# A fused linear-attention and two-layer MoE kernel: routing by groups of six chunks, rows written chunk by chunk from ScalarE's queue, row tiles in the ring of PSUM banks, two conversions on ScalarE

## The chip, the cores and the metric

The kernel runs on one core of one Trainium2 chip. The metric is the device time of one execution in microseconds (us). Before the change the median of three runs is 537.44 us (537.41 to 537.68).

## What is computed

The reference, cut to what matters (4 sequences, 8 heads, 768 steps, head size 48; 3072 tokens of width 384, 8 experts of width 1024):

```python
for t in range(S):                                   # linear attention
    state = alpha[:, :, t, :, None] * state + einsum('bhd,bhe->bhde', k[:, :, t], v[:, :, t])
    y[:, :, t] = einsum('bhd,bhde->bhe', q[:, :, t], state)
x = y.transpose(0, 2, 1, 3).reshape(B * S, H * D)    # 3072 x 384

# MoE 1, only where x @ w_skip > 0; other tokens keep x
e = argmax(x @ w_gate); gate = softmax(x @ w_gate)[e]
x = x + gate * (relu(x @ w1[e]) @ w2[e])

# MoE 2, all tokens, no residual
e = argmax(x @ w_gate2); gate = softmax(x @ w_gate2)[e]
out = gate * (relu(x @ w1b[e]) @ w2b[e])
```

## The kernel before

The work has three stages: the scan with the routing (up to about 160 us), the experts of the first MoE, the experts of the second. The change lies in the first.

The scan handles 24 chunks (NB) of 128 tokens, six for each sequence. The loop at L744 is software-pipelined: iteration g holds pieces of several chunks, and each engine takes its instructions in the order in which they are written. In iteration g stand, one behind the other:

- emit_a(g+1): the products of keys and queries, ap0 and ap1 on PE (L566), each into a bank of PSUM; the causal mask of the first on VectorE (DVE, L574), that of the second on ScalarE (a copy, ACT L571) and GpSimd (POOL L572). Then the keys are transposed on PE (kp, L581) and copied out by ScalarE (ks, L583), except for a sequence's last chunk.
- prep(g+3): the decays. Two scans on DVE (pp L546, qka L550), a reciprocal between them (L548), and two multiplications on POOL (L554, L555).
- emit_y(g): PE adds up the new state (sp, L599, L610, L611) and the chunk's result (yp, L605, L606, L614, L615). ScalarE copies y out (L618), DVE writes the carried state s (L621), which PE reads in the next iteration.
- emit_r(g-1): PE turns y into the tokens' rows of 384 columns and 17 logits (rp, L642). ScalarE copies the rows (xr, L643), DVE adds up the logits (lg, L644).
- the loads of later chunks, v (g+3) and qka (g+5), on SP's queue, which also loads the experts' weights.

PSUM: ap, sp and yp are taken from a ring of four banks ("B"), by the pool as they come free. kp and rp share one further bank ("K", a single buffer), so that kp of an iteration waits until the readers of rp ahead of it have ended: xr on ScalarE, and lg on DVE. Two readers of one bank are also kept apart from each other: lg follows xr. Small routing values lie in one more bank ("own", by spot()).

Routing: the tokens of a group of chunks (GROUPS, eight groups of three) are routed together, by the generator route(i) at L648: cm (L655, L656), a softmax over 8 experts for both layers (L264 to L278; the exponential is ACT's L269), the one-hot choice ohm (L660), the counts and gates (L328 to L289), rank (PE matmuls rk, L312 to L315), positions (L342 to L360), the tables mv (L365) and hot (L372), and the index matmul idx_ps (PE, L377). A group's columns of rows, gate, token number and second logits stand in one tile xr, and SP writes it to the table xrows in DRAM, 394 floats a token (L679). The generators are stepped an instruction at a time by rt() calls between the base instructions of DVE, and how many steps an iteration gets stands in the table RT (L51). Each step is one or a few DVE instructions. Half-weight conversions of the experts (L207, on DVE or POOL) are put in between by release() and background().

After chunk 17 (SPLIT = 6 groups of three) the first index is read and the first expert's rows are gathered by POOL (L441), while the last six chunks go on; after the last chunk the others follow. A gather reads whole rows of xrows, so the writes must have landed.

The constants of the routing are converted in iteration 0, at L757 to L769, on DVE: upper and ones to 16 bit, and small tables copied to PSUM.

Of the kernel before, what the change touches and what calls it, by code (L numbers as in the profile page):

```python
# [8 lines left out]
F32 = mybir.dt.float32  # L9
# [3 lines left out]
AF = mybir.ActivationFunctionType  # L13
ALU = mybir.AluOpType
# [32 lines left out]
GROUPS = [3] * 8  # L47
SPLIT = 6
# [60 lines left out]
def body(tc, qka, vN, rw, wg2, wg17, w1a, w2a, w1b, w2b, cst, zr, out):  # L109
# [3 lines left out]
    with ctx:  # L113
# [21 lines left out]
        with ExitStack() as fctx, tc.manual_schedule():  # L135
# [125 lines left out]
            def softmax_pick(l, n, w, res, scale=1.0):  # L261

                mx = spot("mx", 6, n, w)
                V.tensor_reduce(mx, l, axis=AX.X, op=ALU.max)  # L264
                yield 0
                sh = sm.tile([128, n, w, 8], F32, tag=f"sh{w}", name="sh")
                V.tensor_tensor(sh, l, mx.rearrange("p a (b o) -> p a b o", o=1).to_broadcast([128, n, w, 8]), op=ALU.subtract)
                ex = sm.tile([128, n, w, 8], F32, tag=f"ex{w}", name="ex")
                A.activation(out=ex, in_=sh, func=AF.Exp, scale=scale)  # L269
                yield 0  # L270
                eq = sm.tile([128, n, w, 8], F32, tag=f"eq{w}", name="eq")
                de = kept["desc"].rearrange("p (a e) -> p a e", a=1).to_broadcast([128, n * w, 8])
                V.scalar_tensor_tensor(out=eq.rearrange("p a b e -> p (a b) e"), in0=sh.rearrange("p a b e -> p (a b) e"),
                                       scalar=0.0, in1=de, op0=ALU.is_ge, op1=ALU.mult)
                yield 0
                V.tensor_reduce(mx, eq, axis=AX.X, op=ALU.max)
                yield 0
                V.tensor_tensor(eq, eq, mx.rearrange("p a (b o) -> p a b o", o=1).to_broadcast([128, n, w, 8]), op=ALU.is_equal)  # L278
                res += [eq, ex]
                yield 0  # L280

            def gates(ex, n, w, res):
                den = spot("den", 6, n, w)
# [55 lines left out]
            def index(i, n, nl, ohm, on, rk, cols, region, first, last):  # L339
# [12 lines left out]
                tl = spot("tl", 3, n, 1)  # L352
                V.tensor_reduce(tl[:, :, 0], ge, axis=AX.X, op=ALU.add)
                yield 0
                ti = spot("ti", 24, n, 2, 4)
# [3 lines left out]
                pm = sm.tile([128, n, 1], F32, tag=f"pm{nl}", name="pm")  # L359
# [12 lines left out]
                V.tensor_tensor(hot, kept["iota"].rearrange("p (o c) -> p o c", o=1).to_broadcast([128, n, 128]), pm.to_broadcast([128, n, 128]), op=ALU.is_equal)  # L372
# [261 lines left out]
            def emit_r(g):  # L634

                i, k, n, _ = gof[g]
                if k == 0:
                    xr[i] = em.tile([128, n, ROW], F32, tag="xr", name="xr", bufs=3)
                y = st.pop(("ys", g))
                rp = bank("B" if g == NB - 1 else "K", "rp", NP, 113)  # L640
                for p in range(NP):
                    T.matmul(rp[:, p, :], lhsT=y[:, p, :], rhs=rws[:, p, :], start=True, stop=True)  # L642
                A.activation(out=xr[i][:, k, 0:DM].rearrange("p (a b) -> p a b", a=NP), in_=rp[:, :, 0:96], func=AF.Copy)  # L643
# [4 lines left out]
            def route(i):  # L648
# [5 lines left out]
                cm = spot("cm", 6, n, 2, 1)  # L654
# [9 lines left out]
                def row_ends():  # L664
# [10 lines left out]
                    V.tensor_reduce(x[:, :, GATE], den, axis=AX.X, op=ALU.add)  # L675
                    V.tensor_copy(x[:, :, TOK], kept["tok"][:, g0:g0 + n])
                    V.tensor_tensor(x[:, :, LOG:], l[:, :, 9:17], kept["one"].rearrange("p (a o) -> p a o", o=1).to_broadcast([128, n, 8]), op=ALU.mult)
                    yield 0
                    SY.dma_start(xrows[1 + g0 * 128:1 + (g0 + n) * 128, :].rearrange("(k p) d -> p k d", p=128), x)  # L679
# [64 lines left out]
            for g in range(NB):  # L744
# [11 lines left out]
                if g == 0:  # L756
                    V.tensor_copy(upper, cc("upper"))  # L757
                    V.tensor_copy(ones, cc("ones"))
                    for name, w in (("desc", 8), ("tok", NB), ("iota", 128), ("seq", 8)):
                        kept[name] = spot(name, w, w, bufs=1)  # L760
                        V.tensor_copy(kept[name], cc(name))
# [464 lines left out]
```

## Time and profile before

| | |
|---|---|
| median of three runs | 537.44 us |
| the profiled execution's own time | 539.43 us |
| its span, first to last instruction | 537.70 us |
| PE busy | 496.3 us (92%), 4704 matmuls |
| PE weight loads busy | 381.6 us (71%) |
| DVE busy | 371.5 us (69%), 1031 instructions |
| ScalarE busy | 256.4 us (48%), 466 |
| POOL busy | 262.3 us (49%), 226 |
| granted TensorE clock, mean | 0.981 |

The shares are means over three stages with different limits, so the stage of the scan is read by itself. The page slices the span in 40 (13.4 us each): DVE is at nine tenths or above from the third slice to the tenth, PE at eight tenths or above. From the thirteenth on, DVE falls to three to six tenths and PE stays at nine, which is the stage of the experts. Busy times of PE end where the profile's model puts a matmul's end.

### The profile page before, as it was taken

Reading aid. Unit: us, or ns where it says so; the run is one execution under the profiler, and the core shown is the slowest. Engines: PE = TensorE matmul, PEld = TensorE weight load, DVE = VectorE, ACT = ScalarE, POOL = GpSimd, SP = SyncE. Lnnn points to the kernel's source line nnn. Section 1 sums busy time; section 2 is a strip of 40 time slices with the busy share of each in tenths; the row PEclk is TensorE's granted clock in tenths of the full one; section 3 lists DMA queues with packets and bytes.
Section 4 is the critical chain, followed back from the end, with each engine's and each line's share of the span. In section 5 each row is a group of like instructions: output and inputs, shape, how many; then the busy total and the mean of one; then the engine's idle time right before and its main releaser. Section 6 shows DMA issues by size and latency. Waiting matters only on the chain.

```text
span 537.7 us, 12030 instructions
## 1 busy us (share of the span) xinstructions
PE 496.3 (92%) x4704; PEld 381.6 (71%) x4704; DVE 371.5 (69%) x1031; ACT 256.4 (48%) x466; POOL 262.3 (49%) x226
## 2 busy tenths in 40 slices
PE   5889898998988999999879989999999999999993
PEld 3678787877877899989879757465555566666662
DVE  7978999999876868888768846863636364646320
ACT  1324343444433566566556415653546364646420
POOL 2366958668625666876947341416215150402121
PEclk9989999999999999999989999999999999999997
DMA  8756877425246667676874158473444535360010
GB/s 304 258 190 209 314 250 264 159 114 208 82 173 209 198 249 229 218 260 199 301 245 145 41 196 275 149 244 123 165 147 140 176 118 208 103 223 28 16 39 26
DMA packets 41460, 96.74 MB, mean 180 GB/s; under 512 B 3641, under 2 KB 28471, under 8 KB 41398
## 3 DMA queue, kind: packets, MB, share of 16 engines
q1 hardware_dynamic: 36662, 82.40, 45.0%
q0 software_dynamic: 4736, 13.51, 7.3%
q8 instruction: 39, 0.64, 0.5%
q14 instruction: 23, 0.19, 0.1%
HBM read 83.41 MB, written 12.99 MB: 179 GB/s over the span
## 4 chain that ended last, share of the span: by engine, by line
PE 56%; DVE 28%; DMA 5%; issue 5%; POOL 2%; ACT 2%; POOLq 0%; DVEq 0%; ACTq 0%
PE hp L464 8%; PE hp L463 8%; PE hp L465 8%; DVE pp L546 6%; DVE qka L550 5%; PE ypc L487 4%; PE ypc L488 4%; PE ypc L489 4%; DMA raw<-in_w1a 3%; PE yp L489 3%; PE yp L488 3%; PE yp L487 3%; PE tp L450 3%; POOL w0l L207 2%; DVE at L574 1%
## 5 line engine op out<-in xcount | busy, mean ns | idle before, releaser
L978 POOL DMA_INDIRECT out<-o,ixo x31 | 31.3, 1009 | 142.2 <-ACT o L1051 125.2
L469 DVE SCALAR_TENSOR_TENSOR h2l<-hp,h2h 128x352 f16<-128x352 f32 (+8 forms) x66 | 38.6, 585 | 64.0 <-ACT h2h L468 63.2
L465 PE MATMUL hp<-x2h,w0l 128*128 128x352 f16 (+8 forms) x216 | 68.7, 323 | 0.0
L463 PE MATMUL hp<-x2h,w0h 128*128 128x352 f16 (+8 forms) x216 | 68.7, 323 | 0.0
L464 PE MATMUL hp<-x2l,w0h 128*128 128x352 f16 (+8 forms) x216 | 68.7, 323 | 0.0
L207 POOL TENSOR_TENSOR w1l<-raw,w1h 128x768 bf16<-128x768 f32 (+1 forms) x26 | 43.0, 1681 | 28.2 <-ACT w1h L202 13.7
L463 PE MATMUL hp<-xh,w0h 128*128 128x200 f16 (+7 forms) x216 | 54.0, 257 | 2.5 <-DVE hl L469 1.4
L468 ACT ACTIVATE h2h<-hp 128x352 f16<-128x352 f32 (+8 forms) x66 | 33.8, 513 | 46.9 <-PE hp L465 45.2
L202 ACT ACTIVATE w0h<-raw 128x768 f16<-128x768 f32 x64 | 53.4, 836 | 4.6 <-DMA raw<-in_w1a 2.7
L441 POOL DMA_INDIRECT xg<-xrows,ix x41 | 49.1, 1197 | 11.6 <-issue 9.8
L464 PEld LDWEIGHTS <-w0h 128*128 128x128 f16 x432 | 43.0, 100 | 16.3 <-issue 3.0
L464 PE MATMUL hp<-xl,w0h 128*128 128x200 f16 (+7 forms) x216 | 53.9, 257 | 0.5 <-DVE xl L452 0.3
L465 PEld LDWEIGHTS <-w0l 128*128 128x128 bf16 x432 | 43.0, 100 | 15.6 <-issue 0.7
L465 PE MATMUL hp<-xh,w0l 128*128 128x200 f16 (+7 forms) x216 | 53.9, 257 | 0.0
L488 PE MATMUL yp<-hl,w1h 128*128 128x200 f16 (+7 forms) x216 | 53.4, 255 | 0.5 <-DVE hl L469 0.5
L487 PE MATMUL yp<-hh,w1h 128*128 128x200 f16 (+7 forms) x216 | 53.5, 255 | 0.0
L202 ACT ACTIVATE w1h<-raw 128x768 f16<-128x768 f32 x64 | 51.5, 836 | 4.1 <-DMA raw<-in_w2a 3.8
L489 PE MATMUL yp<-hh,w1l 128*128 128x200 f16 (+7 forms) x216 | 53.4, 255 | 0.0
L463 PEld LDWEIGHTS <-w0h 128*128 128x128 f16 x432 | 43.0, 100 | 13.6 <-issue 0.5
L554 POOL TENSOR_TENSOR qka<-qka 128x512 f32<-128x512 f32 (+1 forms) x24 | 27.5, 1147 | 47.1 <-DVE qka L550 35.7
L207 DVE TENSOR_TENSOR w0l<-raw,w0h 128x768 bf16<-128x768 f32 x38 | 39.7, 1044 | 14.4 <-ACT w0h L202 12.2
L207 POOL TENSOR_TENSOR w0l<-raw,w0h 128x768 bf16<-128x768 f32 (+1 forms) x26 | 43.2, 1685 | 5.0 <-ACT w0h L202 3.8
(183 smaller groups left out, 1346.2 us busy)
## 6 DMA issues: line engine op xcount, KB each, us to landing
qka<-in_qka SPq DMA_DIRECT2D x21, 772.0 KB, 6.0
raw<-in_w1a SPq DMA_DIRECT2D x8, 1536.0 KB, 6.6
raw<-in_w2a SPq DMA_DIRECT2D x8, 1536.0 KB, 9.4
raw<-in_w1b SPq DMA_DIRECT2D x8, 1536.0 KB, 7.9
raw<-in_w2b SPq DMA_DIRECT2D x8, 1536.0 KB, 7.0
xrows<-xr SPq DMA_DIRECT2D x8, 591.0 KB, 3.7
v<-in_vN SPq DMA_DIRECT2D x24, 192.0 KB, 5.1
xrows<-x SPq DMA_DIRECT2D x9, 197.0 KB, 4.1
```

Source lines behind the costliest of these rows:

```text
L202: A.activation(out=hi[:, sl], in_=r[:, sl], func=AF.Copy)
L207: eng.tensor_tensor(lo[:, sl], r[:, sl], hi[:, sl], op=ALU.subtract)
L441: P.indirect_dma_start(out=dst, out_offset=None, in_=xrows[0:rows], in_offset=bass.IndirectOffsetOnAxis(ap=ix, axis=0), bounds_check=rows ...
L463: T.matmul(hp[:, i], lhsT=wh[:, k, f], rhs=xh[:, k, 0:n], start=(k == 0), stop=False)
L464: T.matmul(hp[:, i], lhsT=wh[:, k, f], rhs=xl[:, k, 0:n], start=False, stop=False)
L465: T.matmul(hp[:, i], lhsT=wl[:, k, f], rhs=xh[:, k, 0:n], start=False, stop=(k == 2))
L468: A.activation(out=hh[:, f0:f0 + nf, 0:n], in_=hp, func=AF.Relu)
L469: V.scalar_tensor_tensor(out=hl[:, f0:f0 + nf, 0:n], in0=hp, scalar=0.0, in1=hh[:, f0:f0 + nf, 0:n], op0=ALU.max, op1=ALU.subtract)
L487: T.matmul(yp, lhsT=wh[:, f, ds], rhs=hs[0][:, f, c0:c1], start=(f == 0), stop=False)
L488: T.matmul(yp, lhsT=wh[:, f, ds], rhs=hs[1][:, f, c0:c1], start=False, stop=False)
L489: T.matmul(yp, lhsT=wl[:, f, ds], rhs=hs[0][:, f, c0:c1], start=False, stop=(f == 7))
L546: V.tensor_tensor_scan(pf, a, bz, initial=0.0, op0=ALU.mult, op1=ALU.add)
```

## The change

Four edits, all in the scan stage.

1. GROUPS is [6, 6, 6, 3, 3] and SPLIT is 3, so that the first 18 chunks are three groups and not six. The spots for routing values in PSUM are twice as large. pm moves from SBUF to PSUM, and iota is no longer copied to PSUM: hot compares the constant in SBUF with pm.
2. rp is taken from the ring of four banks, and kp has the bank K alone.
3. ScalarE copies a chunk's 384 columns to a tile xy of its own (four buffers) and starts the DMA that writes them to xrows. The group's tile xr holds the last ten columns alone, 40 bytes a token, which SP writes.
4. The conversions of upper and ones stand on ScalarE.

```diff
-GROUPS = [3] * 8
-SPLIT = 6
+GROUPS = [6, 6, 6, 3, 3]
+SPLIT = 3
...
-                mx = spot("mx", 6, n, w)
+                mx = spot("mx", 12, n, w)
...
-                pm = sm.tile([128, n, 1], F32, tag=f"pm{nl}", name="pm")
+                pm = spot("pm", 6, n, 1)
...
-                V.tensor_tensor(hot, kept["iota"].rearrange("p (o c) -> p o c", o=1).to_broadcast([128, n, 128]), pm.to_broadcast([128, n, 128]), op=ALU.is_equal)
+                V.tensor_tensor(hot, cc("iota").rearrange("p (o c) -> p o c", o=1).to_broadcast([128, n, 128]), pm.to_broadcast([128, n, 128]), op=ALU.is_equal)
...
                 if k == 0:
-                    xr[i] = em.tile([128, n, ROW], F32, tag="xr", name="xr", bufs=3)
+                    xr[i] = em.tile([128, n, ROW - DM], F32, tag="xr", name="xr", bufs=3)
                 y = st.pop(("ys", g))
-                rp = bank("B" if g == NB - 1 else "K", "rp", NP, 113)
+                xy = em.tile([128, DM], F32, tag="xy", name="xy", bufs=4)
+                rp = bank("B", "rp", NP, 113)
                 for p in range(NP):
                     T.matmul(rp[:, p, :], lhsT=y[:, p, :], rhs=rws[:, p, :], start=True, stop=True)
-                A.activation(out=xr[i][:, k, 0:DM].rearrange("p (a b) -> p a b", a=NP), in_=rp[:, :, 0:96], func=AF.Copy)
+                A.activation(out=xy.rearrange("p (a b) -> p a b", a=NP), in_=rp[:, :, 0:96], func=AF.Copy)
+                A.dma_start(xrows[1 + g * 128:1 + (g + 1) * 128, 0:DM], xy)
...
-                    V.tensor_reduce(x[:, :, GATE], den, axis=AX.X, op=ALU.add)
-                    V.tensor_copy(x[:, :, TOK], kept["tok"][:, g0:g0 + n])
+                    V.tensor_reduce(x[:, :, GATE - DM], den, axis=AX.X, op=ALU.add)
+                    V.tensor_copy(x[:, :, TOK - DM], kept["tok"][:, g0:g0 + n])
...
-                    SY.dma_start(xrows[1 + g0 * 128:1 + (g0 + n) * 128, :].rearrange("(k p) d -> p k d", p=128), x)
+                    SY.dma_start(xrows[1 + g0 * 128:1 + (g0 + n) * 128, DM:].rearrange("(k p) d -> p k d", p=128), x)
...
-                    V.tensor_copy(upper, cc("upper"))
-                    V.tensor_copy(ones, cc("ones"))
-                    for name, w in (("desc", 8), ("tok", NB), ("iota", 128), ("seq", 8)):
+                    A.activation(out=upper, in_=cc("upper"), func=AF.Copy)
+                    A.activation(out=ones, in_=cc("ones"), func=AF.Copy)
+                    for name, w in (("desc", 8), ("tok", NB), ("seq", 8)):
```

Lines behind L642 shift by one or two: lg is L646 after the change, xy L644, its DMA L645.

How the instructions stand, at three places. First DVE at the end of iteration 0; the names are those of tiles, out <- in. Before:

```order
L621 TENSOR_TENSOR s<-sp,pp 128x192
L757 CAST upper<-cs 128x128
L758 CAST ones<-cs 128x128
L761 COPY own<-cs 128x8
L761 COPY own<-cs 128x24
L761 COPY own<-cs 128x128
```

The same engine and place after the change:

```order
L621 TENSOR_TENSOR s<-sp,pp 128x192
L763 COPY own<-cs 128x8
L763 COPY own<-cs 128x24
L763 COPY own<-cs 128x8
L766 COPY own<-cs 128x4
```

Two conversions and the copy of iota have left the row. They stand now on ScalarE, ahead of iteration 1's mask copy, where also the first xy and its DMA are seen, at the end of iteration 1:

```order
L618 ACTIVATE y<-yp 112x512
L759 ACTIVATE upper<-cs 128x128
L760 ACTIVATE ones<-cs 128x128
L571 ACTIVATE at<-ap_271 128x512
L583 ACTIVATE ks<-kp 128x512
L618 ACTIVATE y<-yp 112x512
L644 ACTIVATE xy<-rp 128x384
L645 DMA xrows<-xy 128x384
```

The DMA stands behind the copy it waits for, and ahead of the next iteration's mask copy and ks.

Second, DVE where a group's table hot is done and the next chunks follow. Before, at the end of the routing of chunks 3 to 5, in iteration 8:

```order
L372 TENSOR_TENSOR hot<-own,pm 128x384
L207 TENSOR_TENSOR w0l_727<-raw_0_490,w0h_726 128x768
L574 TENSOR_TENSOR at<-ap_916,cs 128x512
L546 SCALAR_TENSOR_TENSOR pp<-qka,bz 128x520
L548 RECIPROCAL bz_113<-pp 128x4
L550 SCALAR_TENSOR_TENSOR qka<-qka,bz_113 128x520
L621 TENSOR_TENSOR s<-sp,pp 128x192
L644 TENSOR_REDUCE lg<-rp 128x17
L655 TENSOR_SCALAR own<-lg 128x3
L656 TENSOR_SCALAR own<-lg 128x3
L264 TENSOR_REDUCE own<-lg 128x6
L574 TENSOR_TENSOR at<-ap_992,cs 128x512
```

After, at the end of the routing of chunks 0 to 5, also in iteration 8:

```order
L372 TENSOR_TENSOR hot<-cs,own 128x768
L207 TENSOR_TENSOR w0l_688<-raw_0_492,w0h_687 128x768
L574 TENSOR_TENSOR at<-ap_883,cs 128x512
L546 SCALAR_TENSOR_TENSOR pp<-qka,bz 128x520
L548 RECIPROCAL bz_113<-pp 128x4
L550 SCALAR_TENSOR_TENSOR qka<-qka,bz_113 128x520
L621 TENSOR_TENSOR s<-sp,pp 128x192
L646 TENSOR_REDUCE lg<-rp 128x17
L574 TENSOR_TENSOR at<-ap_961,cs 128x512
L546 SCALAR_TENSOR_TENSOR pp<-qka,bz 128x520
```

Before, the next group begins with the next chunk. After, routing stands in iterations 6 (three instructions), 7 (eleven) and 8 (thirteen), then in none up to the end of iteration 12, where the next group begins; that one stands in 13 to 15, and the third in 19 and 20. From chunk 20 on, the order is that of before except for widths. Weight splits (L207) stand at the ends of iterations 8, 12, 16 and 20.

Third, PE around chunk 10, with what each instruction waits for (Activation is ScalarE, Pool GpSimd, DMAHW a DMA queue). Before:

```order
L642 MATMUL rp<-rws,y 128x113 [waits Activation_49]
L642 MATMUL rp<-rws,y 128x113 x3
L566 MATMUL ap_916<-qka 128x128 [waits DMAHW6_49,Pool_49]
L566 MATMUL ap_917<-qka 128x128 [waits DVE_49]
L566 MATMUL ap_916<-qka 128x128
L566 MATMUL ap_917<-qka 128x128
L566 MATMUL ap_916<-qka 128x128
L566 MATMUL ap_917<-qka 128x128
L566 MATMUL ap_916<-qka 128x128
L566 MATMUL ap_917<-qka 128x128
L581 MATMUL kp<-cs,qka 128x128 [waits DVE_49]
L581 MATMUL kp<-cs,qka 128x128 x3
```

After:

```order
L643 MATMUL rp<-rws,y 128x113 [waits Activation_49]
L643 MATMUL rp<-rws,y 128x113 x3
L566 MATMUL ap_883<-qka 128x128 [waits DMAHW1_49,DVE_49,Pool_49]
L566 MATMUL ap_884<-qka 128x128 [waits DVE_49]
L566 MATMUL ap_883<-qka 128x128
L566 MATMUL ap_884<-qka 128x128
L566 MATMUL ap_883<-qka 128x128
L566 MATMUL ap_884<-qka 128x128
L566 MATMUL ap_883<-qka 128x128
L566 MATMUL ap_884<-qka 128x128
L581 MATMUL kp<-cs,qka 128x128 [waits Activation_49]
L581 MATMUL kp<-cs,qka 128x128 x3
```

kp waited for DVE in every iteration; after the change it waits for ScalarE (ks of the chunk before) or for nothing. In about 12 of the last 20 iterations one or both of the ap tiles wait for DVE, which has to read the bank's last tile first.

## Rows read from the trace of the kernel before

**Rows 1.** Windows by stage: bounds, length, busy PE, PEld, DVE, ACT, POOL (instructions); clock, DMA share, GB/s.

```profile
34.00:54.40 20.40, 20.18 (x283) 17.36 (x280) 16.41 (x48) 9.26 (x18) 12.48 (x15) 1.00 0.71 246
54.40:124.10 69.70, 64.03 (x887) 54.99 (x886) 67.91 (x182) 30.66 (x57) 50.52 (x40) 1.00 0.63 222
124.10:153.20 29.10, 27.27 (x377) 23.50 (x376) 24.12 (x82) 12.92 (x26) 18.41 (x16) 1.00 0.36 128
```

**Rows 2.** All of L581 (kp): what PE idled for, us and times.

```profile
  DVE lg L644: 16.8, 21
```

**Rows 3.** Timeline of DVE, iterations 0 and 1: start us, duration us, engine, line, operation, tiles.

```profile
21.44 1.18 DVE L757 CAST upper<-cs 128x128 f16<-128x128 f32 x1
22.54 1.22 DVE L758 CAST ones<-cs 128x128 f16<-128x128 f32 x1
...
25.31 0.69 DVE L574 TENSOR_TENSOR at<-ap,cs 128x512 f32<-128x512 f32 x1
...
28.80 0.22 DVE L644 TENSOR_REDUCE lg<-rp 128x17 f32<-128x68 f32 x1
```

**Rows 4.** Timeline of PE, same stretch; in brackets the idle time before and its releaser.

```profile
29.07 1.04 PE L581 MATMUL kp<-cs,qka 128*128 128x128 f32 x4 [1.87 <-DVE lg L644]
```

**Rows 5.** Groups of PE instructions, 54.4 to 124.1: count, busy us, mean ns, idle before.

```profile
L377 PE MATMUL idx_ps<-mv,hot 128*128 128x96 f16 x15 | 1.5, 209 | 0.2
...
L315 PE MATMUL rk<-cum,ones 128*128 128x48 f16 x4 | 0.7, 183 | 0.0
```

**Rows 6.** Groups of DVE instructions by form, 20 to 160 us, columns as before.

```profile
L546 DVE TENSOR_TENSOR_SCAN pp<-qka,bz 128x520 f32<-128x520 f32 x20 | 31.3, 1565 | 0.0
L550 DVE TENSOR_TENSOR_SCAN qka<-qka,bz 128x520 f32<-128x520 f32 x21 | 29.0, 1379 | 0.6
L574 DVE TENSOR_TENSOR at<-ap,cs 128x512 f32<-128x512 f32 x20 | 13.6, 681 | 0.4 <-PE ap L566 0.3
L621 DVE TENSOR_TENSOR s<-sp,pp 128x192 f32<-128x192 f32 x20 | 6.8, 338 | 0.2
L644 DVE TENSOR_REDUCE lg<-rp 128x17 f32<-128x68 f32 x24 | 5.3, 220 | 6.7 <-ACT xr L643 6.7
...
L548 DVE RECIPROCAL bz<-pp 128x4 f32<-128x4 f32 x20 | 3.5, 176 | 0.3
...
L365 DVE TENSOR_TENSOR mv<-on,own 128x192 f16<-128x192 f16 x7 | 2.4, 346 | 0.0
...
L365 DVE TENSOR_TENSOR mv<-on,own 128x96 f16<-128x96 f16 x7 | 1.7, 242 | 0.0
```

**Rows 7.** Timeline of DVE in a later iteration, around chunk 15.

```profile
105.59 2.65 DVE L546 TENSOR_TENSOR_SCAN pp<-qka,bz 128x520 f32<-128x520 f32 x1
...
109.68 0.33 DVE L621 TENSOR_TENSOR s<-sp,pp 128x192 f32<-128x192 f32 x1
```

**Rows 8.** All of L679 (SP writes xr): ns min/median/max, first and last start; landing.

```profile
L679 SPq EVENT_SEMAPHORE x8: 4868/9852/13631, 40.2 to 155.5; - x8
L679 SPq DMA_DIRECT2D xrows<-xr x8: 383/394/399, 48.8 to 160.4; - x8
...
DMA to landing us min/median/max: 3.4/3.7/5.4
```

**Rows 9.** Timeline of all engines, 33.5 to 41 us: ScalarE and DVE in one iteration.

```profile
35.27 0.49 ACT L643 ACTIVATE xr<-rp 128x384 f32<-128x384 f32 x1 [0.41 <-PE rp L642]
35.79 0.23 DVE L644 TENSOR_REDUCE lg<-rp 128x17 f32<-128x68 f32 x1 [2.23 <-ACT xr L643]
...
36.45 0.60 ACT L571 ACTIVATE at<-ap 128x512 f32<-128x512 f32 x1 [0.70 <-PE ap L566]
```

**Rows 10.** Timeline of POOL at the end of the stage: the gather behind the last write.

```profile
166.13 1.02 POOL L441 DMA_INDIRECT xg<-xrows,ixb  x1 [8.80 <-DVE own L700]
```

**Rows 11.** Timeline of PE in the iteration of rows 7.

```profile
108.52 1.16 PE L566 MATMUL ap<-qka 64*128 64x128 f32 x16
```

More of the change, by code (lines that the diff above doesn't have):

```diff
@@ L282, in gates @@
             def gates(ex, n, w, res):
-                den = spot("den", 6, n, w)
+                den = spot("den", 12, n, w)
                 V.tensor_reduce(den, ex, axis=AX.X, op=ALU.add)
@@ L350, in index @@
                 yield 0
-                tl = spot("tl", 3, n, 1)
+                tl = spot("tl", 6, n, 1)
                 V.tensor_reduce(tl[:, :, 0], ge, axis=AX.X, op=ALU.add)
                 yield 0
-                ti = spot("ti", 24, n, 2, 4)
+                ti = spot("ti", 48, n, 2, 4)
                 V.tensor_tensor(ti, cc("seq")[:, 0:4].rearrange("p (a o e) -> p a o e", a=1, o=1).to_broadcast([128, n, 2, 4]),
@@ L653, in route @@
                 res = []
-                cm = spot("cm", 6, n, 2, 1)
+                cm = spot("cm", 12, n, 2, 1)
                 V.tensor_scalar(cm[:, :, 0, :], l[:, :, 0:1], 0.0, None, op0=ALU.is_gt)
@@ L674, in row_ends @@
                     yield 0
-                    V.tensor_reduce(x[:, :, GATE], den, axis=AX.X, op=ALU.add)
-                    V.tensor_copy(x[:, :, TOK], kept["tok"][:, g0:g0 + n])
-                    V.tensor_tensor(x[:, :, LOG:], l[:, :, 9:17], kept["one"].rearrange("p (a o) -> p a o", o=1).to_broadcast([128, n, 8]), op=ALU.mult)
+                    V.tensor_reduce(x[:, :, GATE - DM], den, axis=AX.X, op=ALU.add)
+                    V.tensor_copy(x[:, :, TOK - DM], kept["tok"][:, g0:g0 + n])
+                    V.tensor_tensor(x[:, :, LOG - DM:], l[:, :, 9:17], kept["one"].rearrange("p (a o) -> p a o", o=1).to_broadcast([128, n, 8]), op=ALU.mult)
                     yield 0
-                    SY.dma_start(xrows[1 + g0 * 128:1 + (g0 + n) * 128, :].rearrange("(k p) d -> p k d", p=128), x)
+                    SY.dma_start(xrows[1 + g0 * 128:1 + (g0 + n) * 128, DM:].rearrange("(k p) d -> p k d", p=128), x)
                 side = [start(row_ends())]
```

## The prediction

> **What bounds the kernel now.** I read the windows by stage first, then the order of the instructions, then the timelines of single iterations. The change lies in the first 160 us, where the scan loop runs with its routing, so only those stages count.
>
> The windows begin where a chunk's rp begins. From 34.0 to 54.4 us, four iterations, PE is busy 20.18 of 20.40 us and DVE 16.41: PE sets the pace, at 20.2 / 4 = 5.05 us an iteration [rows 1]. From 54.4 to 124.1, twelve iterations and four routing groups, DVE is busy 67.91 of 69.70 and PE 64.03: DVE sets the pace and PE has 5.7 us of waiting, nearly all of it in front of the kp transposes, which wait for DVE's logit reduction lg (16.8 us in 21 waits over the whole loop) [rows 1, 2]. From 124.1 to 153.2 both have holes, PE 1.8 us and DVE 5.0 [rows 1]. Behind 153.2 stand the expert networks, which the change leaves as they are.
>
> So a gain must be a DVE instruction less where DVE is full, or a PE wait less where PE is not. An iteration is a loop in lockstep: PE's ap feeds DVE's mask, and the carried state s, at the end of DVE's share, feeds the next matmuls. Neither engine can run a whole iteration ahead of the other.
>
> **Part 1: the constants converted on ScalarE (start).** In iteration 0 DVE converts upper and ones, 1.18 and 1.22 us, and copies the constants behind them; its next mask starts at 25.31 [rows 3]. A little later PE stands 1.87 us in front of kp, until lg is done at 28.80 + 0.22 us [rows 3, 4]. After the change the DVE row runs from s straight to the small copies, shorter by 2.4 us and by the iota copy. ScalarE takes the two conversions while it waits for PE. kp waits for lg no more, as rp leaves its bank, so PE can gain the 1.87 us of that wait and not much more. Value −1.9; bounds 0 (something else of DVE's is late there) and −2.7 (all that DVE is spared).
>
> **Part 2: fewer groups of routing.** *Iterations 3 to 6 (34.0 to 54.4 us).* PE-bound, and the first group's rank and index matmuls are gone from them: idx is 1.5 us for 15, so 0.3 for a group, and one kind of rank matmul 0.7 us for four, 0.18 each, of which a group has four [rows 5]: about 1.0 together, partly under neighbours. Value −0.4, bounds 0 and −1.0.
>
> *Iterations 7 to 18 (54.4 to 124.1).* A chunk's share of DVE: scans 1.565 and 1.379, mask 0.681, state 0.338, lg 0.220, reciprocal 0.176 us, together 4.36 [rows 6]. Instructions overlap: 21.44 + 1.18 is 22.62, and the next starts at 22.54 [rows 3]; six times 0.08 off leaves 3.9 a chunk, 46.8 for twelve. Of the 67.9 busy us [rows 1] 21.1 remain: three weight splits that the order puts there, taken at a scan's 1.3 each, and four groups, 4.3 us a group. A group of six costs more per instruction: mv takes 242 ns for 96 columns and 346 for 192 [rows 6], 1.08 ns a column; hot grows by 384 columns, mv by 96 and 192, on by 96, the dozen softmax and rank tensors by 48 or less, some 1,340 columns or 1.45 us. So a group of six costs 5.75 where two of three cost 8.6: DVE is spared 2.85 us per six chunks, 5.7 in all.
>
> What reaches the end is less, since the order makes the load uneven. Routing is stepped out at the old rate, so a group of six is through after about three iterations, and the other three have base work alone. With the in-place base at 4.0 (the scans stretched a little) the routing iterations of the first six take 3 × 4.0 + 5.75 + a split of 1.3 = 19.05, DVE-bound; the other three fall to PE's 5.05 each, 15.15. Together 34.2. The second six has its three routing iterations at 19.5 and comes to 34.65. Sum 68.85 for 69.70: value −0.9. Bounds −5.7, if the slack evens out across iterations, and +3, if scans stretch as the one of 2.65 us did [rows 7].
>
> *From iteration 19.* The group of chunks 12 to 17 is now six wide: +1.45 us of DVE where three wide stood. DVE is busy 24.12 of 29.10 there [rows 1], so part is hidden: +0.9, bounds 0 and +1.45. The last two groups of three are as before.
>
> **Part 3: rows and logits in the ring of banks.** The wait of kp for lg, 16.8 us in 21 [rows 2], goes. It is not a saving of 16.8: where DVE is full, PE waits for DVE a few matmuls later instead. Its share at the start is in part 1; elsewhere 0, bounds inside those of part 2. The price is that five tiles an iteration share four banks where four did. By the order ap then waits for a DVE reader in some 12 of the last 20 iterations. That is the slower rival below; 0 here.
>
> **Part 4: rows written from ScalarE's queue.** 24 more DMA issues on ScalarE; one on SP's queue takes 383 to 399 ns [rows 8]. Behind each stand the next at (the second half's mask copy) and ks. ScalarE is busy 30.66 of 69.70 us [rows 1], and after xr it idles 0.70 us for ap before at [rows 9], longer than an issue. Value 0; the bound, all of them on the path, is 24 × 0.4 = +9.6, taken far off since the row shows the cover. If the ring makes ap late, the cover grows.
>
> The group's remaining write is now 40 bytes a token, 768 pieces for six chunks. On SP's queue the write waits 4.9 to 13.6 us for the routing, with loads behind it [rows 8]; there are five such waits now for eight, and the row of loads runs ahead by two chunks or more: 0. The old write landed after 3.4 to 5.4 us, the last issued at 160.4 [rows 8]; the gather that needs it is issued at 166.13 [rows 10]. Even 5.4 gives 165.8: 0; bound +1.7, for a landing of twice the median (160.4 + 7.4 − 166.1). The Trainium skill, DMA: Bandwidth & Descriptors, § Specifications, puts the size for full rate at 512 bytes and over, with a read-modify-write below; by it the landing would lie nearer that bound, and the sum would be up to 1.7 more. No row here shows writes as small as these.
>
> hot now reads iota from SBUF and pm from PSUM, still one operand in PSUM as the mask has, whose 681 ns for 512 [rows 6] is the usual rate: 0.
>
> **Sum.** −1.9 − 0.4 − 0.9 + 0.9 = −2.3. The profiled execution took 539.43 us, 2.0 above the median; −2.3 gives 537.1 against it and **535.1** against the median of 537.44.
>
> **Rivals.**
>
> *PE has more room than its busy time says.* Then all 5.7 us of DVE's saving counts in place of 0.9: 535.1 − 4.8 = 530.3. For it: PE's weight loads are busy 54.99 of 69.70 only [rows 1], and PE's 5.7 us of waiting are just as many. Against it: at 34.0 to 54.4 us iterations take 5.05 us with PE never waiting and DVE waiting 2.23 in one place [rows 1, 9]. The Trainium skill, Perfetto Trace Analysis, § Identifying the Most-Contended Engine, calls matmul busy time a poor measure and weight-load busy share a better one; by it PE is at 79% and this rival holds. The trace speaks against it with the 5.05 us. Chance 0.17.
>
> *The ring of banks, slower.* A loop closes through the banks: ap waits until s, the last of DVE's chunk, has read its bank; then ap, mask, scan, scan, s. In one iteration before, ap starts at 108.52 and s ends at 109.68 + 0.33, 1.5 us later [rows 7, 11]: ap could run ahead of s, and with the ring it can't. That exposes ap's time, which one piece of a timeline has at 1.16 us [rows 11], in iterations bound by DVE. Six of the twelve have routing, and with 12 in 20 that is 3.6 waits, 3.6 × 1.16 = +4.2: 539.3. It decides from the point where such a loop passes PE's 5.05: 1.16 + 0.6 + scan + 0.1 + 1.3 + 0.3, so from a first scan of 1.6 us, about the mean of today's [rows 6]. Against it: s has moved earlier in the iterations without routing, and banks are taken as they come free, so that not every loop closes. Chance 0.18.
>
> *The unevenness eats it.* Iterations with routing lose what the others win, and at the start another wait takes half of the 1.9: −0.9 + 0 + 0.9, so 537.4, no change. For it: PE-bound iterations were already within 1 us of DVE's. Chance 0.22.
>
> **How the numbers follow.** Forecast 0.43, around 533 to 537. A measurement here tells about 0.2% from no change, 1.1 us. Faster: 0.37 of the forecast's, all 0.17 of the first rival's and 0.03 of the third's, 0.57. Slower: 0.16 of the ring's, 0.01 of the third's. Same: the rest, 0.26. The range goes from the first rival's 530.3 to 540.0, past the ring's 539.3; half of either rival and the forecast's tail lie outside, under 0.2.
>
> **What would show it.** Part 1: no PE wait in front of kp near 29 us, and the fifth rp at 52 instead of 54.4. Part 2: rp to rp near 6.3 us in routing iterations and 5.05 in the others, about 68.9 for the twelve. Part 3: waits of PE ap for DVE s; if they add up to several us, the ring rival holds. Part 4: the ScalarE queue shows no wait between its DMA and at, and the small write lands before the last gather. I am wrong if iterations without routing also take 5.5 us or more, or if they fall well below 5.

## The result and the profile after

Measured together on one chip, eight runs each, the kernel before takes 538.64 us (median, 537.41 to 540.39) and the changed one 533.74 (532.96 to 535.38). The ratio is 0.9912, 95% interval 0.9897 to 0.9927: 4.7 us faster, where 2.3 were forecast. The profiled execution of the changed kernel took 533.13 us, span 531.3; that of before, 539.43, was a longer than usual one, so the two traces stand 6.3 us apart where the medians stand 4.9.

The page of the changed kernel, its busy times (DVE had 1031 instructions):

```profile
PE 494.6 (93%) x4701; PEld 380.5 (72%) x4701; DVE 365.4 (69%) x947; ACT 256.5 (48%) x465; POOL 268.1 (50%) x226
```

The stages, cut at the same rp as in [rows 1] (its columns): first rp to second (iteration 2; the expectations call it iteration 1), then iterations 3 to 6, 7 to 18, 19 to 23.

```profile
24.76:30.32 5.56, 5.56 (x81) 4.87 (x79) 5.21 (x9) 2.17 (x4) 4.38 (x4) 1.00 0.67 216
30.32:50.26 19.94, 19.94 (x274) 17.35 (x273) 15.25 (x23) 8.80 (x17) 16.38 (x16) 1.00 0.94 318
50.26:119.06 68.80, 65.51 (x886) 56.48 (x883) 63.93 (x128) 30.09 (x55) 50.05 (x39) 1.00 0.72 232
119.06:146.37 27.31, 26.66 (x373) 22.75 (x370) 23.72 (x78) 12.83 (x25) 20.93 (x17) 1.00 0.25 70
```

The same cuts in before:

```profile
24.64:34.08 9.44, 7.57 (x80) 6.56 (x78) 8.54 (x15) 2.28 (x4) 5.36 (x4) 0.82 0.33 106
34.08:54.41 20.33, 20.11 (x282) 17.38 (x280) 16.42 (x48) 9.27 (x18) 12.41 (x15) 1.00 0.71 247
54.41:124.13 69.72, 64.05 (x888) 55.01 (x886) 67.93 (x182) 30.68 (x57) 50.54 (x40) 1.00 0.63 222
124.13:152.06 27.93, 26.10 (x366) 22.33 (x365) 23.59 (x80) 12.50 (x25) 18.38 (x16) 1.00 0.34 119
```

Read by length: 9.44 to 5.56 (−3.88, forecast −1.9), 20.33 to 19.94 (−0.39, forecast −0.4), 69.72 to 68.80 (−0.92, forecast −0.9), 27.93 to 27.31 (−0.62, forecast +0.9). Behind the last of these cuts the experts' stages take 385.6 us before and 384.9 after, 0.7 us that no term of the forecast holds. So two of the four terms came out, and the surplus stands at the start, and behind 119 us.

At the start the timeline of the changed kernel's PE shows kp without a wait and at full speed, where [rows 4] has 1.87 us of waiting and 1.04 us for the same four transposes:

```profile
25.84 1.16 PE L566 MATMUL ap<-qka 64*128 64x128 f32 x16
26.93 0.66 PE L581 MATMUL kp<-cs,qka 128*128 128x128 f32 x4
```

DVE's row there (compare [rows 3]) has its mask at 22.87 us for 25.31 before, and lg at 26.60 for 28.80:

```profile
22.87 0.69 DVE L574 TENSOR_TENSOR at<-ap,cs 128x512 f32<-128x512 f32 x1
...
26.60 0.22 DVE L646 TENSOR_REDUCE lg<-rp 128x17 f32<-128x68 f32 x1
```

The 1.87 us wait is half of the 3.88. The other half is the clock: before, the granted clock is 1.00 in 24 to 28 us and 0.65 in 28 to 32, behind the wait; in the changed kernel it is 1.00 there. (The value is a mean over the window: in 30 to 32 us alone it is 0.50 before, the lower of the two levels, 1.2 of 2.4 GHz.) The same matmuls then take up to twice as long, in a stretch where PE is the one that is late. That the wait brings the clock down is what the filler and the rows below bear out.

### The profile page after: what moved, and what is told of

Its sections match the earlier page's. It is cut to its first block, busy times and chain, and to the rows that moved or that the text cites. A ratio compares the mean times of both kernels' runs of the same rounds, so it can differ in the third digit from the quotient of the medians.

```text
span 531.3 us, 11974 instructions
## 1 busy us (share of the span) xinstructions
PE 494.6 (93%) x4701; PEld 380.5 (72%) x4701; DVE 365.4 (69%) x947; ACT 256.5 (48%) x465; POOL 268.1 (50%) x226
## 4 chain that ended last, share of the span: by engine, by line
PE 66%; DVE 21%; DMA 5%; issue 4%; ACT 2%; POOL 1%; POOLq 0%; ACTq 0%; DVEq 0%
PE hp L463 8%; PE hp L464 8%; PE hp L465 8%; PE ypc L487 4%; PE ypc L488 4%; PE ypc L489 4%; DVE qka L550 4%; DVE pp L546 4%; PE ap L566 3%; DMA raw<-in_w1a 3%; PE yp L488 3%; PE tp L450 3%; PE yp L489 3%; PE yp L487 3%; PE rp L643 3%
## 5 line engine op out<-in xcount | busy, mean ns | idle before, releaser
L463 PE MATMUL hp<-xh,w0h 128*128 128x200 f16 (+7 forms) x216 | 52.4, 252 | 5.3 <-DVE hl L469 4.4
L207 POOL TENSOR_TENSOR w1l<-raw,w1h 128x768 bf16<-128x768 f32 (+1 forms) x26 | 43.0, 1683 | 27.0 <-ACT w1h L202 16.6
L464 PEld LDWEIGHTS <-w0h 128*128 128x128 f16 x432 | 42.3, 98 | 19.1 <-issue 5.7
L464 PE MATMUL hp<-xl,w0h 128*128 128x200 f16 (+7 forms) x216 | 52.3, 252 | 0.1
L465 PE MATMUL hp<-xh,w0l 128*128 128x200 f16 (+7 forms) x216 | 52.3, 252 | 0.0
L463 PEld LDWEIGHTS <-w0h 128*128 128x128 f16 x432 | 42.3, 98 | 13.6 <-issue 0.5
L207 DVE TENSOR_TENSOR w0l<-raw,w0h 128x768 bf16<-128x768 f32 x38 | 39.6, 1043 | 13.1 <-ACT w0h L202 11.0
L207 POOL TENSOR_TENSOR w0l<-raw,w0h 128x768 bf16<-128x768 f32 (+1 forms) x26 | 44.1, 1720 | 4.9 <-ACT w0h L202 2.7
```

What stands on the lines that cost most here:

```text
L207: eng.tensor_tensor(lo[:, sl], r[:, sl], hi[:, sl], op=ALU.subtract)
L463: T.matmul(hp[:, i], lhsT=wh[:, k, f], rhs=xh[:, k, 0:n], start=(k == 0), stop=False)
L464: T.matmul(hp[:, i], lhsT=wh[:, k, f], rhs=xl[:, k, 0:n], start=False, stop=False)
L465: T.matmul(hp[:, i], lhsT=wl[:, k, f], rhs=xh[:, k, 0:n], start=False, stop=(k == 2))
```

## Experiments

Each kernel was timed against the kernel before in the same session (538.2 to 538.9 us). What the profiles give, from rp to rp, in us:

| kernel | median | ratio to before, 95% | first to second rp | 3 to 6 | 7 to 18 | 19 to 23 |
|---|---|---|---|---|---|---|
| before | 538.6 | | 9.44 | 20.33 | 69.72 | 27.93 |
| changed | 533.74 | 0.9912 (0.9897 to 0.9927) | 5.56 | 19.94 | 68.80 | 27.31 |
| before, conversions on ScalarE | 537.05 | 0.9966 (0.9949 to 0.9983) | 5.56 | 20.66 | 69.71 | 27.94 |
| before, rp in the ring | 541.07 | 1.0040 (1.0022 to 1.0057) | 7.29 | 21.41 | 71.80 | 29.71 |
| before, filler in the wait | 537.88 | 0.9984 (0.9969 to 0.9999) | 7.83 | 19.96 | 70.08 | 27.92 |
| before, rows from ScalarE | 538.71 | 0.9992 (0.9976 to 1.0008) | 6.22 | 20.66 | 69.78 | 27.93 |
| before, groups and rows | 537.72 | 0.9971 (0.9952 to 0.9989) | 9.12 | 19.73 | 68.66 | 27.71 |
| changed, rp in bank K | 535.54 | 0.9943 (0.9921 to 0.9965) | 5.56 | 19.73 | 68.94 | 27.72 |
| changed, rows from SP | 539.60 | 1.0009 (0.9992 to 1.0026) | 5.56 | 19.96 | 74.79 | 27.27 |
| changed, routing spread | 537.20 | 0.9977 (0.9962 to 0.9992) | 5.56 | 19.72 | 73.04 | 27.28 |
| changed, conversions on DVE | 536.36 | 0.9961 (0.9944 to 0.9979) | 6.96 | 20.45 | 68.79 | 27.31 |
| changed, one copy on ScalarE | 529.99 | 0.9849 (0.9824 to 0.9874) | 5.56 | 19.94 | 68.80 | 27.30 |
| the same, filler at the start | 530.29 | 0.9860 (0.9836 to 0.9883) | 6.44 | 19.73 | 68.66 | 27.31 |
| the same copy, rp in bank K | 530.71 | 0.9856 (0.9823 to 0.9888) | 5.56 | 19.73 | 69.01 | 27.72 |

(A profile is one execution. Iterations 19 to 23 and mostly 7 to 18 agree to 0.1 us between kernels that have them in common, but not always: kernels with the iterations of before took 19.96 to 20.66 us in 3 to 6 and 69.71 to 70.08 in 7 to 18, with the clock at 1.00. So a few tenths in one cell of the table say nothing.)

**The conversions alone.**

```diff
-                    V.tensor_copy(upper, cc("upper"))
-                    V.tensor_copy(ones, cc("ones"))
+                    A.activation(out=upper, in_=cc("upper"), func=AF.Copy)
+                    A.activation(out=ones, in_=cc("ones"), func=AF.Copy)
```

> The kernel before with one edit: upper and ones are converted on ScalarE. In iteration 1 of before (from the first rp at 24.64 us to the second at 34.08, 9.44 us, 5.56 in the changed kernel) PE waits 1.87 us for lg, and then runs some 3.5 us at the lower clock level. Theory: DVE's late row is the whole cause; lg ends near 27.1 us, kp waits 0.3 us at most, the clock stays up, and the second rp comes near 30.5: -3.5 us against before, about 0.9935 of it. Rival 1, the shared bank K is the cause: kp still waits over a microsecond and the gain is under 1.5 us. Rival 2, the clock falls whatever the wait is: only the wait goes, -1.9 us.

The time from the first rp to the second falls from 9.44 to 5.56 us, all that the whole change gives there, with the bank still shared: rival 1 falls. The median moves by 1.8 us only (by the ratio; 0.9 to 2.7), not 3.5. Part of the reason can be read in the clock of 13 to 24 us in this execution:

```profile
13.00:16.00 3.00, 2.98 (x20) 2.44 (x22) 2.93 (x4) 1.19 (x2) 0.00 (x0) 0.50 1.04 414
16.00:20.00 4.00, 3.92 (x40) 3.53 (x38) 3.93 (x7) 0.99 (x3) 1.69 (x2) 0.50 1.01 353
20.00:24.00 4.00, 4.00 (x40) 3.10 (x38) 3.72 (x13) 1.19 (x2) 2.51 (x3) 0.63 0.52 193
```

The low clock of the start lies at 13 to 23 us here, where before's profile had 0.58, 1.00 and 1.00, and the first rp came at 25.30 for 24.64, so the second came 3.2 us earlier and not 3.9. Where the low clock lies differs between executions whose instructions up to there are the same; the profile of before was one in which it struck twice, at 13 and behind the wait at 29, and at 539.43 us it is slower than the median of its kernel. How often it strikes behind the wait in executions without a profile is not shown.

**The ring alone.**

```diff
-                rp = bank("B" if g == NB - 1 else "K", "rp", NP, 113)
+                rp = bank("B", "rp", NP, 113)
```

> The kernel before with one edit: rp of every chunk lies in the ring of four banks, kp alone in bank K. Theory (the start is DVE's lateness, and from 54 us on DVE sets the pace): kp waits no more, but sp behind it waits for DVE's s, which ends at 28.88 us, so PE's wait in iteration 1 shrinks only from 1.87 to about 1.2 us, the clock may still fall, and the twelve iterations from 54.4 us stay within 1 us of 69.7: 0 to -1.5 us in all. Rival, the bank is the cause: kp's 16.8 us of waits were on the path, iteration 1 falls below 7 us and the total by 3 us or more. Second rival, the ring binds: ap waits for s in iterations full of DVE work, +1 to +4 us.

The second rival, the slower one of the prediction: 2.2 us slower, with groups of three. PE's waits of ap for s are there, 3.6 us in the twelve iterations, and behind one of them the clock is at 0.67 (64 to 68 us), which makes that iteration 9.26 us. The same happens once more in iterations 19 to 23: a wait of 1.59 us at 134.14, the clock at 0.71 in 136 to 140 us, again 9.26 us. At the start PE passes kp and waits 1.09 us at sp for s, and behind that the clock stays at 1.00. The waits, the matmuls, and the window:

```profile
PE ap L566 <- DVE s L621: 3.6, 4, 1.6
```

```profile
62.58 1.54 PE L566 MATMUL ap<-qka 64*128 64x128 f32 x14 [1.59 <-DVE s L621]
```

```profile
64.00:68.00 4.00, 4.00 (x49) 3.46 (x50) 3.86 (x11) 1.19 (x2) 2.72 (x3) 0.67 0.55 169
```

In the changed kernel the same wait sums to 2.0 us in the twelve, none over 1.24, and the clock stays at 1.00. What disarms it can be told from four of these runs. With groups of three the ring costs 2.2 us (1.0040). With groups of six and chunked rows, conversions on DVE in both, the kernel takes 0.9971 of before without the ring and 0.9961 with it: no cost that can be told. So it is the groups and rows together; that it is the groups is likely, since the rows alone changed nothing, but no run has the ring with the groups and without the rows.

**A filler in PE's wait.**

```diff
+                if g == 3:
+                    wq = bank("M", "wq", 512)
+                    for i in range(7):
+                        T.matmul(wq, lhsT=warm[:, 0:128], rhs=warm[:, 128:640], start=True, stop=True)
                 if g % NC < NC - 1:
                     kp = bank("K", "kp", NP, GP)
```

> The kernel before with seven more matmuls of zeros (512 columns, 16 bit, results unused), put in front of the transposes kp of iteration 2's preparation, where PE waits 1.87 us for DVE. They stand in the wait and take nothing away from it. Theory (a wait of PE is followed by some 3.5 us at the lower clock level, which costs about 2 us on top): the second rp comes some 2 us earlier, near 32.1 us, with the clock at the upper level in 30 to 33 us: -2 us. Rival, the fall of the clock belongs to something else (a later wait, or it comes anyway): 0, or +0.5 if the filler is late itself.

28 to 32 us before, and with the filler:

```profile
28.00:32.00 4.00, 2.93 (x18) 2.49 (x20) 3.93 (x7) 0.60 (x1) 3.28 (x3) 0.65 0.09 37
```

```profile
28.00:32.00 4.00, 3.75 (x52) 2.83 (x52) 3.93 (x7) 0.60 (x1) 3.27 (x3) 1.00 0.10 38
```

With the wait left as it is, work of no use in it keeps the clock at 1.00, and the time from the first rp to the second is 1.6 us shorter (7.83). So the fall does belong to the wait, and costs about as much again. In the median 0.9 us is left (0.1 to 1.7), where 2 were expected; that not every execution has the second fall would explain it, and is not shown.

**The rows alone.**

```diff
...
-                A.activation(out=xr[i][:, k, 0:DM].rearrange("p (a b) -> p a b", a=NP), in_=rp[:, :, 0:96], func=AF.Copy)
+                A.activation(out=xy.rearrange("p (a b) -> p a b", a=NP), in_=rp[:, :, 0:96], func=AF.Copy)
+                A.dma_start(xrows[1 + g * 128:1 + (g + 1) * 128, 0:DM], xy)
...
```

> The kernel before with one edit: each chunk's 384 columns are copied to a tile of their own and written from ScalarE's queue, and the group's write from SP holds 40 bytes a token. Theory: the issues, 0.34 us each, lie in ScalarE's waits for ap, and the small writes land in about 3 us: 0, within 1 us. Rival: the issues stand in front of the mask copy in iterations that have no slack, 24 x 0.34 = up to +8 us; a quarter of it would be +2.

No difference, and its iterations are before's to 0.1 us from the seventh on. This execution has the low clock at the start in 8 to 18 and in 22 to 25 us, and then none at 28 to 32. So PE comes to kp later, the first rp at 26.32, and waits 0.60 us there and not 1.87. lg is no earlier than in before (28.88 for 28.80) and kp starts at 29.16 for 29.07, and yet the second rp stands at 32.54 for 34.08: without the fall of the clock the same matmuls from the same point on are 1.6 us shorter, the filler's price once more. First to second rp is 6.22 us, and this is the spread that makes one profile of a start a poor price for it.

```profile
29.16 0.66 PE L581 MATMUL kp<-cs,qka 128*128 128x128 f32 x4 [0.60 <-DVE lg L646]
```

**Groups of six and rows, with bank K shared and DVE's conversions.**

```diff
-GROUPS = [3] * 8
-SPLIT = 6
+GROUPS = [6, 6, 6, 3, 3]
+SPLIT = 3
...
```

> The kernel before with groups of six (and the spots, pm and iota that go with them) and the rows written from ScalarE's queue, without which the group's tile does not fit; bank K stays shared, the conversions stay on DVE. Theory: the start stays as in before but for the iota copy (second rp within 0.5 us of 34.08), iterations 3 to 6 give 0.4, iterations 7 to 18 give 0.9 as in the changed kernel, the stretch behind gives nothing or loses 0.9: -0.5 to -1.5 us in all. Rival, the groups carry the gain: -3 us or more.

About as expected: 1.1 us less in iterations 7 to 18, 0.6 in 3 to 6, and in all 1.05 by the medians, 1.6 by the ratio (0.6 to 2.6). It doesn't carry the gain alone. kp's wait of 1.87 us at the start is still there, and so is the clock behind it, 0.62 in 28 to 32 us.

**The changed kernel with rp in bank K.**

> The changed kernel with rp put back into bank K beside kp. Theory: the start keeps its gain, since lg is early enough (second rp within 0.4 us of 30.32); in iterations without routing kp waits for lg again, some tenths each, and in the stretch behind 119 us the 1.5 us come back that the forecast missed there: +1 to +2.5 us against the changed kernel. Rival, the ring gives nothing (a wait of ap for s stands where kp's stood): within 0.5 us of the changed kernel.

The medians give 1.8 us to the ring, but the intervals overlap, and the iterations differ by 0.3 us in all (68.94 and 68.80, 27.72 and 27.31, the other way in 3 to 6). kp waits for lg for 9.9 us in this kernel, 16.8 in before, and that is nearly all hidden. The last kernel below compares the same pair once more.

**The changed kernel with the rows from SP.**

```diff
-                A.dma_start(xrows[1 + g * 128:1 + (g + 1) * 128, 0:DM], xy)
+                SY.dma_start(xrows[1 + g * 128:1 + (g + 1) * 128, 0:DM], xy)
```

> The changed kernel with the chunk's rows written from SP's queue in place of ScalarE's. Theory: each write waits on SP for its copy with the loads of later chunks and weights behind it, as the group's write did in before; the loads run ahead by two chunks, so 0 within 1 us. Rival: the loads of weights are late behind 24 more waits, and the experts' stage starts later: +2 us or more.

The rival, and not with the weights but with the scan's own loads: 5 to 6 us more than the changed kernel (by the ratios and the medians), all of it in iterations 7 to 18, with 8.30 and 9.36 us in the first two and 9.35 in iteration 14. What waits there:

```profile
POOL qka L554 <- DMA v<-in_vN: 5.3, 1, 5.3
...
DVE pp L546 <- DMA qka<-in_qka: 3.7, 2, 3.5
...
PE sp L599 <- DVE s L621: 2.8, 2, 2.5
```

SP's queue stood 91.8 us in 21 waits for ScalarE's copies over the whole execution, the longest 11.3, and the loads of later chunks stand behind them. So ScalarE's queue gives nothing over before's groups, but it is what lets a write for each chunk cost nothing. One row here speaks against a simple price of a wait: PE waits 2.48 us for s at 55.48, and the clock stays at 1.00 in 54 to 60 us; it falls behind the waits of 1.66 us at 61.70 and 1.58 us at 98.06, to 0.50 in 62 to 64 and in 100 to 102.

```profile
55.48 0.59 PE L599 MATMUL sp<-s,cs 128*128 128x192 f32 x2 [2.48 <-DVE s L621]
```

**The routing spread evenly.**

```diff
...
             def rt(n=1):
                 for _ in range(n):
+                    if left[0] <= 0:
+                        return
+                    left[0] -= 1
...
             for g in range(NB):
+                left[0] = 4 if 6 < g < 18 else 10**9
```

> The changed kernel with a cap of four routing steps by the calls inside an iteration in iterations 7 to 17, so that a group of six is routed over five iterations (about 7, 5, 6, 5, 5 of DVE's instructions between two lg) and not three (9, 13, 6). The work is the same. Theory (the unevenness takes most of DVE's saving): iterations 7 to 18 go from 68.8 us to about 66, where PE is never waiting: -2 to -3 us against the changed kernel. Rival (PE's need is what stands there already, or DVE's scans stretch instead): within 0.7 us of it.

The kernel is slower than the changed one (0.9977 for 0.9912), and my theory of the unevenness falls, at least in its size. The first six of the twelve, more evenly loaded now, take 34.2 us for 33.95. Of the second six the first five take 29.6 for 30.6, so an us is gained there; in the last (9.25 us for 4.22) the index matmul now stands in front of ap and waits 3.03 us for hot, with the clock at 0.66 in 119 to 124 us:

```profile
119.34 0.43 PE L381 MATMUL idx_ps<-mv,hot 128*128 128x96 f16 x6 [3.03 <-DVE hot L376]
119.70 1.52 PE L570 MATMUL ap<-qka 64*128 64x128 f32 x16
```

The eighth iteration is 7.38 us with 13 DVE instructions in it, 7.47 with 22 without the cap. What stands in it is seen in the changed kernel: both scans, 1.23 us where POOL is idle, take 1.76 and 2.19 beside POOL's weight split, and ap waits for s behind them.

```profile
53.85 1.76 DVE L546 TENSOR_TENSOR_SCAN pp<-qka,bz 128x520 f32<-128x520 f32 x1
...
55.96 2.19 DVE L550 TENSOR_TENSOR_SCAN qka<-qka,bz 128x520 f32<-128x520 f32 x1
```

```profile
54.47 2.58 POOL L207 TENSOR_TENSOR w0l<-raw,w0h 128x768 bf16<-128x768 f32 x1
```

```profile
58.62 1.16 PE L566 MATMUL ap<-qka 64*128 64x128 f32 x14 [1.24 <-DVE s L621]
```

**The changed kernel with the conversions back on DVE.**

> The changed kernel with the conversions of upper and ones back on DVE; ring, groups and rows stay as changed. Theory (DVE's late row in iteration 1 makes PE wait whatever the bank is): with kp alone in its bank PE passes kp and waits at sp for s, some 1.2 us, and then runs at the lower clock level: iteration 1 near 7.3 us as with the ring alone (5.56 in the changed kernel), +1.5 to +3.5 us against the changed kernel. Rival, the ring alone is enough when the routing is thin: iteration 1 under 6 us and within 0.7 us of the changed kernel.

The theory in time, but not in all of its mechanism: first to second rp is 6.96 us, the next iteration longer too (5.91), and PE waits 1.09 us at sp for s in place of 1.87 at kp, but the clock behind that wait stays at 1.00 in 28 to 36 us. 2.6 us slower than the changed kernel. So the conversions are worth 1.8 us in before and 2.6 here, two values that the intervals don't tell apart, and the free bank does not do their work.

**A version that beats both: one copy moved.** In the changed kernel's trace the next large wait of PE stands in the first expert's stage, at 171.40 us. Ahead of it DVE copies eight 16-bit columns in 3.53 us (2.22 in before), while POOL runs three weight splits:

```profile
165.70 3.53 DVE L967 COPY cum<-cum 128x8 f16<-128x8 f16 x1
```

```profile
164.35 4.84 POOL L207 TENSOR_TENSOR w0l<-raw,w0h 128x769 bf16<-128x769 f32 x3
```

```profile
171.40 0.20 PE L463 MATMUL hp<-xh,w0h 128*128 128x80 f16 x1 [3.50 <-DVE hl L469]
```

The copy ends at 169.23 and the splits at 169.19. The Trainium skill, SBUF — State Buffer, § Who interferes with whom, says that a copy on VectorE in a two-port mode takes the port pair that it shares with GpSimd for a whole instruction, and that whoever comes second is blocked. The rows agree with the blocking: the copy came second and ended with the splits, and so it did, within 0.1 us, in all eleven kernels that have it on DVE. That the copy ran in such a mode no row shows.

```diff
-                    V.tensor_copy(cum2[:, 0, :], cum[:, len(GROUPS), 8:16])
+                    A.activation(out=cum2[:, 0, :], in_=cum[:, len(GROUPS), 8:16], func=AF.Copy)
```

> The changed kernel with one copy of eight 16-bit columns (the counts, between the two layers, L967) moved from DVE to ScalarE. In the changed kernel it stands 3.53 us on DVE and ends when POOL ends three weight splits (169.23 us), in the one before 2.22 us; PE waits 3.50 us behind it and runs at 0.70 to 0.83 of its clock up to 178 us. Theory (the copy waits for POOL, DVE for the copy, PE for DVE, and the clock falls behind the wait): PE's wait goes and with it the low clock: -3 to -6 us against the changed kernel. Rival, the next DVE instruction or ScalarE's copy is held as long: within 1 us.

529.99 us, 3.4 (by the ratios) to 3.8 us (by the medians) below the changed kernel. The copy takes 0.20 us on ScalarE. 164 to 171 and 171 to 178 us, in the changed kernel and then in this one:

```profile
164.00:171.00 7.00, 3.23 (x69) 3.06 (x70) 5.85 (x9) 0.99 (x4) 6.51 (x6) 1.00 0.30 67
171.00:178.00 7.00, 6.44 (x103) 6.00 (x103) 5.56 (x31) 4.95 (x12) 3.11 (x4) 0.76 0.67 268
```

```profile
164.00:171.00 7.00, 6.20 (x136) 5.89 (x137) 5.45 (x26) 3.23 (x11) 6.51 (x6) 1.00 0.28 72
171.00:178.00 7.00, 6.50 (x85) 5.75 (x83) 5.52 (x21) 4.63 (x10) 6.84 (x6) 1.00 0.82 309
```

PE is busy 6.20 us for 3.23 in the first, and the clock of the second is 1.00 for 0.76.

**The same, with a filler in the wait ahead of the second ap.**

```diff
+                if g == 1:
+                    wq = bank("M", "wq", 512)
+                    for i in range(10):
+                        T.matmul(wq, lhsT=warm[:, 0:128], rhs=warm[:, 128:640], start=True, stop=True)
                 ap = [bank("B", f"ap{h}", NP, C) for h in range(2)]
```

> As the run with the copy on ScalarE, and ten more matmuls of zeros (512 columns, results unused) in PE's wait of 2.50 us ahead of the second ap (9.64 to 12.14 us), behind which the clock is at 0.51 in 13 to 16 us. Theory: the low clock at 12 to 16 us goes; DVE sets the pace there (9.75 of 13.4 us, then 6.46 of 6.6), so the first rp comes at most 0.5 us earlier, and 0 to -1 us against the run without the filler. Rival, the low clock only moves to a later place: 0 to +1.5 us.

Inconclusive in time (530.29 and 529.99). The clock is at 1.00 in every window from 0 to 36 us, and the first rp comes at 24.64 for 24.71: DVE sets the pace there, and a clock has no price where PE isn't late. First to second rp is 6.44 us in this execution, where ap waits 0.40 us for s, which it doesn't in the run without the filler; the rest of that 0.9 us stays open.

**The same copy, with rp in bank K.**

> The kernel with the copy on ScalarE (529.99 us, ratio 0.9849 to before) with rp put back into bank K beside kp. The changed kernel with K had a median 1.8 us above the changed kernel's (535.54 and 533.74), but its iterations sum to 0.2 us of the same time up to the last rp. Theory (the ring gives next to nothing by itself in the final kernel, the medians differ by where the low clock fell): ratio 0.984 to 0.987. Rival (the ring is worth its 1.8 us): 0.988 or above.

Ratio 0.9856 (0.9823 to 0.9888) against 0.9849 (0.9824 to 0.9874): what the ring itself gives in the final kernel isn't told from nothing, nor from the 1.8 us of the medians above. In iterations 19 to 23 all three kernels of this kind with bank K take 27.7 us, with the ring 27.3.

## Why the prediction was right, point by point

The direction, and the range, held: 533.7 in 530.3 to 540.0, for 535.1. The gain was twice the forecast's, and the terms say why. That the range had room is partly luck: two terms left their own bounds (the start −2.7, the stretch from iteration 19 zero), both to the fast side, and the lower end stood at 530.3 for the sake of the first rival, which did not come.

**Part 1, the start: right mechanism, price too small.** The step that failed is "PE can gain the 1.87 us of that wait and not much more". The trace gave 3.88 in the profiled pair, beyond the bound of 2.7, since the wait's end is not the end of its cost: matmuls behind it ran at the lower clock level. [Rows 4] had it in its duration, kp at 1.04 us for 0.66 elsewhere. The filler shows that part alone (−1.6 in the iteration). Across executions the whole edit is worth 1.8 us in before and 2.6 in the changed kernel. (The rp forecast at 52 us for 54.4 is the sixth, not the fifth; it came at 50.26.)

**Part 2, iterations 3 to 18: right sums, the reason for one of them not shown.** −0.39 and −0.92 for −0.4 and −0.9. The first match is partly luck, since other executions of the same iterations spread over 0.7 us. (By the page of before DVE is at nine tenths from the fifth to the tenth slice, 54 to 134 us, and not from the third; that iterations 3 to 6 are PE's agrees with it.) DVE's busy time fell by 4.0 us in the twelve iterations, 5.7 were expected; the scans took part of it back (L550 18.1 us for 16.1, L546 20.5 for 21.3). The unevenness, on which I put the difference between the saving and the gain, is not shown to be its cause: evening it out gave 0 in one six and 1 us in five iterations of the other, where 2 to 3 were due. In the eighth iteration what stands in the way is the scan beside POOL's split and ap's wait for s; for the others this stays open.

The prediction named a sign of being wrong, iterations without routing well below 5 us, and it was there: iterations 12 and 18 take 4.30 and 4.22 us, 5.83 each before. PE is busy all the time in them (4.51 and 4.50 of 5.83 before). They hold the first chunk of a sequence, which has no carried state, so that the matmuls with s are missing. PE's 5.05 us was a mean over unlike iterations, 5.56 to 4.22 in the changed kernel's 3 to 6, and not one pace for all. The two gave 3.1 us, and the other ten together lost 2.2 of it, up to 1.1 in one with routing.

**Part 2, from iteration 19: the wrong sign.** +0.9 forecast, −0.6 measured. I had put the 1.45 us of the wider group on the path. DVE's busy time in the stretch grew by 0.13 us only (23.72 for 23.59), and DVE isn't what is late: PE is busy 26.66 of 27.31 us, 26.10 of 27.93 before, and it lost waits. With groups of six and bank K the stretch is 27.7 us, with the ring 27.3.

**Part 3, the ring: the rival's mechanism is real, and was disarmed.** Alone it made the kernel before 2.2 us slower, by the wait of ap for s that I had named and its low clock. In the changed kernel it costs 2.0 us of waits and saves kp's, and the sum is not told from zero. The prediction's reason why not every loop closes, s earlier in iterations without routing, fits the pair of runs with groups of six, where the ring has no cost that can be told.

**Part 4, the rows: 0, as forecast.** An issue took 0.34 us on ScalarE; the 40-byte writes landed in 2.9 us, faster than [rows 8], the last of them, issued at 154.9, before the gather at 160.71. So the Trainium skill's warning on small writes (DMA: Bandwidth & Descriptors, § Specifications) is not seen at up to 768 pieces:

```profile
L681 SPq DMA_DIRECT2D xrows<-xr x5: 388/394/398, 61.2 to 154.9; - x5
...
DMA to landing us min/median/max: 2.9/2.9/2.9
```

**The first rival** (PE has room) did not hold as a whole: the weight loads are busy 56.48 of 68.80 us, 82%, and the twelve iterations gave 0.9 us and not 5.7. In the two iterations of 4.30 and 4.22 us PE did have the room. **The third rival** (no change) is excluded by the interval.

## What to carry to other kernels

Price a wait of TensorE with the granted clock of the stretch behind it: where PE is the late engine there, most waits of 1.6 to 3.0 us cost 1 to 2 us more than themselves in these runs (one of 2.48 us did not, and its clock stayed up), waits up to 1.24 us in the changed kernel's scan did not, and where another engine is late, the clock cost nothing. Take a start's price from several executions, since the low clock moves. An edit can be a loss alone (the ring, +2.2 us) and none beside another; and a write for each chunk belongs on a queue that no load stands in.

## What the runs showed of the hardware that was not expected

A copy of eight 16-bit columns stood 2.1 to 3.9 us on DVE in all eleven kernels that have it there, each time to within 0.1 us of the end of POOL's splits; on ScalarE it took 0.20 us in the other three. And a stretch of lower clock at the start lay between 12 and 17 us in most profiles, at 13 to 23 or at 18 to 25 in others, or was split (8 to 18 and 22 to 25), in executions whose instructions up to there are nearly the same; the whole run's mean clock went from 0.978 to 0.987 over the eight runs of the changed kernel, and its time from 535.38 to 533.13 us.
